# A sliding-window attention with a gated block on one core: first loads regrouped, block 0 handled in three pieces, five POOL drains

## The chip, the cores and the metric

The kernel runs on one core of a Trainium2 chip. The metric is device time in microseconds (us), the median of several executions. Every execution quoted here is fast, with a granted TensorE clock of 0.995 to 1.0. Engines are PE (matmul), PEld (its weight loads), DVE (vector), ACT (scalar), POOL (GpSimd) and SP (here only a queue that issues DMAs). All times inside an execution are counted from the start of its span, which is the stretch from the first to the last instruction of the profiled execution.

## The reference

```python
x = A_x                                   # (1, 2048, 512), bf16
xn = layernorm(x)                         # over the 512 columns, no weights
qkv = xn @ wqkv                           # 512 -> 3*512; 32 heads of 16
o = softmax(q k^T / 4, causal, window 256) v
h = (x @ w_gate) * (x @ w_up)             # 1792 wide; the kernel uses xn, see below
return x + o @ wo + h @ w_down
```

In the real text the second branch is called as `_B_ref(xn, ...)`, so both branches read the normalised `xn`. The output is 2048 x 512 in bf16. The tokens are handled in 4 chunks of 512 (`T`), each chunk in 4 blocks of 128 tokens (`b`).

## The kernel before

The kernel is written as a list of operations with dependencies. A small planner in Python walks the list while the kernel is built: it has estimates of when loads land and how long each operation takes, and it emits instructions in the order in which its plan starts them. The order on each engine is therefore fixed when the kernel is built, and the numbers of the plan decide it.

The first loads are issued on two queues, SP and ACT:

```python
load(nc.sync, self.Wqkv[:, 0:2, 1024:1536], ...)      # value weights, first half
load(nc.scalar, self.x[:, 0, :], xv[:, 0, :])         # x0: block 0 of x
load(nc.sync, self.Wqkv[:, 2:4, 1024:1536], ...)      # value weights, second half
load(nc.scalar, self.x[:, 1, :], xv[:, 1, :])         # x1
for t, lo in ((2, 512), (3, 0)):                      # key weights, x2; query weights, x3
    load(nc.sync, self.Wqkv[:, :, lo:lo + 512], ...)
    load(nc.sync, self.x[:, t, :], xv[:, t, :])
# ... gate and up weights, x4 to x15 ...
for f, g in ((0, 4), (4, 8), (8, 11), (11, 14)):
    load(nc.sync, self.Wd[:, f:g], w["d"][:, f:g])
load(nc.sync, self.Wo[:], w["o"])
for _ in range(4):
    nc.sync.drain()
# ... constants on POOL, DVE and ACT ...
nc.gpsimd.memset(self.V[0][:, :, :, 16:18], 1.0)
self.keep_busy(42, 0)                                 # 42 idle matmuls on PE
```

For every block of chunk 0 DVE takes statistics, ACT a square root, DVE a reciprocal, and DVE scales the block. PE turns it (four 128 x 128 transposes into a PSUM bank), and DVE or ACT copies the turned block to `xnT`. Then come the value, key and query matmuls. Keys are copied out twice ("lanes"), each time with half of the heads zeroed:

```python
land = (3.4, 3.95, 7.7, 9.6)              # the plan: when x0 to x3 land
wv, wk, wq = 5.9, 7.3, 9.3                # ... and value, key and query weights
# ...
parts = 2 if b == 0 else 1                # block 0 is scaled in halves
for n in range(parts):
    cols = slice(n * 512 // parts, (n + 1) * 512 // parts)
    # ... one op on DVE: i_apply(b, cols)
# ...
def k_out(o, i, b=b):                     # o: the matmuls, i: their bank
    x = o
    for lane in range(2):                 # lane 1 waits for lane 0
        x = self.op(f"K0b{b}", PSUM_COPY, [o, x], lambda e, lane=lane: self.i_keys(...))
    self.frees(x, i)                      # the bank is free after lane 1
# ...
for n, ks in enumerate(([0, 1], [2, 3]) if b == 0 else ([0, 1, 2, 3],)):
    self.A.insert(at + n, Dense(f"turn{b}", ...))     # block 0 is turned in halves
```

All turns, projections and later matmuls take one of four PSUM banks `M[0..3]`, whichever the plan has had free the longest:

```python
def take_bank(self):
    i = min((t, i) for i, t in enumerate(self.banks) if t is not None)[1]
    self.banks[i] = None
    return i
```

The last output block is summed and stored in two halves, the first on SP, the second on ACT:

```python
queue = "A" if cols.start else "S"
self.op(f"out{t}", {queue: (0.6, 2.2)}, [x], lambda e: (
    self.nc.scalar if cols.start else self.nc.sync).dma_start(
    out=self.out_d[128 * t:128 * t + 128, cols], in_=keep["y"][:, cols]), rank=0)
```

The softmax here doesn't subtract the row's maximum and nothing guards it: scores larger than these inputs give would overflow.

Of the kernel before, what the change touches and what calls it, by code (L numbers as in the profile page):

```python
# [50 lines left out]
def layout(T):  # L51


    if T == 0:
        return [[(2, 2, 4, 0), (4, 4, 4, 4)], [(0, 0, 5, 0), (5, 5, 3, 5)],
                [(1, 1, 5, 0), (6, 6, 2, 5), (7, 7, 1, 7)], [(3, 3, 5, 0), (2, 6, 1, 5)]]
    return [[(3, 3, 5, 0), (-3, 0, 2, 5), (-4, 0, 1, 7)], [(2, 2, 5, 0), (6, 6, 2, 5), (7, 7, 1, 7)],
            [(0, 0, 5, 0), (5, 5, 3, 5)], [(1, 1, 5, 0), (-2, 0, 3, 5)], [(-1, 0, 4, 0), (4, 4, 4, 4)]]
# [27 lines left out]
class Kernel:  # L86
# [56 lines left out]
    def prologue(self):  # L143
        nc = self.nc
        xv = self.x_d.rearrange("(t p) d -> p t d", p=128)
        w = {k: v.rearrange("(k p) n -> p k n", p=128) for k, v in self.w_d.items()}

        def load(eng, dst, src):
            eng.dma_start(out=dst, in_=src)  # L149

        load(nc.sync, self.Wqkv[:, 0:2, 1024:1536], w["qkv"][:, 0:2, 1024:1536])
        load(nc.scalar, self.x[:, 0, :], xv[:, 0, :])
        load(nc.sync, self.Wqkv[:, 2:4, 1024:1536], w["qkv"][:, 2:4, 1024:1536])
        load(nc.scalar, self.x[:, 1, :], xv[:, 1, :])
        for t, lo in ((2, 512), (3, 0)):
            load(nc.sync, self.Wqkv[:, :, lo:lo + 512], w["qkv"][:, :, lo:lo + 512])
            load(nc.sync, self.x[:, t, :], xv[:, t, :])
        h = self.F // 2
        for lo in (0, h):
            load(nc.sync, self.Wg[:, :, lo:lo + h], w["g"][:, :, lo:lo + h])  # L160
            load(nc.sync, self.Wu[:, :, lo:lo + h], w["u"][:, :, lo:lo + h])
            if lo == 0:
                load(nc.sync, self.x[:, 4:8, :], xv[:, 4:8, :])
        load(nc.sync, self.x[:, 8:NT, :], xv[:, 8:NT, :])
# [6 lines that stand above are left out]
        c = self.const  # L171
        nc.gpsimd.memset(self.ident[:], 0.0)
        nc.gpsimd.affine_select(out=self.ident[:], in_=self.ident[:], compare_op=ALU.not_equal, fill=1.0,
                                base=0, pattern=[[-1, 128]], channel_multiplier=1)
        nc.gpsimd.memset(self.mhalf[:], -0.5)
        warm = c.tile([128, 1], F32, name="warm")
        nc.vector.memset(warm[:], 0.0)
        nc.vector.memset(self.eps[:], 1e-5)
        nc.scalar.activation(out=warm[:], in_=warm[:], func=ACT.Sqrt)
        self.warm = warm  # L180
        pi = c.tile([128, 1], I32, name="pi")
        nc.gpsimd.iota(pi[:], pattern=[[0, 1]], base=0, channel_multiplier=1)
        podd = c.tile([128, 1], I32, name="podd")
        nc.vector.tensor_scalar(out=podd[:], in0=pi[:], scalar1=4, scalar2=1,
                                op0=ALU.arith_shift_right, op1=ALU.bitwise_and)
        nc.vector.tensor_copy(out=self.own[:, 1:2], in_=podd[:])
        nc.vector.tensor_scalar(out=self.own[:, 0:1], in0=podd[:], scalar1=0, scalar2=None, op0=ALU.is_equal)
        nc.gpsimd.memset(self.V[0][:, :, :, 16:18], 1.0)
        self.keep_busy(42, 0)


# [96 lines left out]
    def run(self):  # L288
        if self.live:
            self.prologue()  # L290
        self.now, self.mode = 5.4, "D"
        self.free = {"V": 3.0, "A": 4.5, "G": 3.0, "S": 6.0}
        self.waiting, self.log, self.idle = [], [], []
        self.banks = [0.0] * 4
        self.s_free, self.p_free = 0.0, [0.0] * self.PBUFS
        self.at_ = {}
        self.A, self.B = [], []
        self.g = self.v = 0
        self.first_s = None
        self.credit = 0.0  # L300
        self.pairs = [(T, c) for T in range(NCH) for c in range(4)]
        self.batches, self.of_pair = [], []
        for T, c in self.pairs:
            batches = layout(T)
            self.of_pair.append(range(len(self.batches), len(self.batches) + len(batches)))
            self.batches += [(T, c, b) for b in batches]
        self.list_work()
        self.loop()
        return max(self.now, *self.free.values(), *(o for o in self.at_.values() if isinstance(o, float)))
# [263 lines left out]
    def psT(self, i):  # L573
        return self.M[i].bitcast(BF16)[:, 0:512].rearrange("p (k t) -> p k t", k=4)

    def first_chunk(self):

        land = (3.4, 3.95, 7.7, 9.6)
        wv, wk, wq = 5.9, 7.3, 9.3
        nc = self.nc  # L580
        roots = []
        for b in range(4):
            keep = {}

            halves = 2 if b == 1 else 1

            def bn(e, n, b=b, keep=keep, halves=halves):
                if n == 0:
                    keep["st"] = self.work.tile([128, 2, 6], F32, tag="st", name="st")
                cols = slice(n * 512 // halves, (n + 1) * 512 // halves)  # L590
                nc.vector.bn_stats(out=keep["st"][:, n, :], in_=self.x[:, b, cols])  # L591
                if n == halves - 1:
                    nc.vector.bn_aggr(out=self.mv[0][:, b, :], in_=keep["st"][:, 0:halves, :])

            deps = [land[b]]
            for n in range(halves):
                took = (0.72 if halves == 1 else 0.38) + (0.14 if n == halves - 1 else 0)
                s = self.op(f"st{b}", {"V": (took, took + 0.04)}, deps, lambda e, n=n, bn=bn: bn(e, n), rank=0.5)
                deps = [self.at_["ap", 0, 0], s] if b == 1 else deps
            s = self.op(f"sq{b}", {"A": (0.24, 0.25)}, [s], lambda e, b=b: nc.scalar.activation(  # L600
                out=self.ve[:, b:b + 1], in_=self.mv[0][:, b, 1:2], func=ACT.Sqrt, bias=self.eps[:]), rank=0)
            roots.append(s)
            s = self.op(f"rs{b}", {"V": (0.15, 0.16)}, [s], lambda e, b=b: nc.vector.reciprocal(  # L603
                out=self.rs[0][:, b:b + 1], in_=self.ve[:, b:b + 1]), rank=0)
            parts = 2 if b == 0 else 1
            for n in range(parts):
                cols = slice(n * 512 // parts, (n + 1) * 512 // parts)
                took = (0.38, 0.48) if parts == 1 else (0.22, 0.30)
                self.at_["ap", b, n] = self.op(f"ap{b}", {"V": took}, [s], lambda e, b=b, cols=cols: self.i_apply(b, cols), rank=0)
        self.op("table", {"A": (1.5, 1.5)}, roots + [("Q", 0, 0, 2)], lambda e: nc.scalar.activation(  # L610
            out=self.warm[:], in_=self.warm[:], func=ACT.Exp), rank=1)
        last = self.op("masks", {"V": (0.15, 0.2)}, [self.at_["ap", 1, 0]], lambda e: nc.vector.memset(self.masks[:], -1), rank=9)
# [6 lines left out]
        for b in range(4):  # L619
            tok = slice(128 * b, 128 * b + 128)  # L620

            def turn(i, ks, b=b):
                for k in ks:
                    self.nc.tensor.transpose(self.psT(i)[:, k, :], self.xn[b][:, 128 * k:128 * k + 128], self.ident[:])  # L624
                if b == 0:
                    self.keep_busy(2 * ks[0], 3)

            def turned(o, i, ks, b=b, tok=tok):
                took = {"A": (0.48, 0.6), "V": (0.31, 0.41)} if len(ks) == 4 else {"A": (0.27, 0.38)}
                ks = slice(ks[0], ks[-1] + 1)  # L630
                x = self.op(f"xT{b}", took, [o], lambda e: self.copy(e, self.xnT[0][:, ks, tok], self.psT(i)[:, ks]), rank=0)
                self.frees(x, i)
                self.at_["xnT", 0, b] = self.at_["xnT", 0, b, ks.start] = x
                x.then.append(lambda o: self.at_.update({("begun", 0, b, ks.start): o.start}))
# [20 lines left out]
                    self.at_["Q", 0, c, b] = x  # L655

            at = len(self.A) - 2 if b else 0
            for n, ks in enumerate(([0, 1], [2, 3]) if b == 0 else ([0, 1, 2, 3],)):
                self.A.insert(at + n, Dense(f"turn{b}", 1.3 * len(ks) / 4, [("ap", b, n)], lambda i, f=turn, ks=ks: f(i, ks),
                                            lambda o, i, f=turned, ks=ks: f(o, i, ks)))  # L660
            self.add_v(0, b, wv)
# [171 lines left out]
```

## Time and profile before

| | before |
|---|---|
| time, median of 3 executions | 265.99 us (265.85 to 266.75) |
| time beside the change later, median of 6 | 265.89 us (265.64 to 266.75) |
| span of the profiled execution | 264.0 us |
| first value matmul / first key matmul of block 0 | 6.29 / 7.63 us |
| first score matmul | 17.33 us |
| end of DVE's last output sum | 261.03 us |
| from there to the end of the span ("the tail") | 2.95 us |

These lines are from the page of the kernel before: the span, each engine's busy time with its share and its instructions, the shares of the chain that ended last, and three of the DMA queues (packets, MB, share of 16 engines). Queues of the kind "instruction" fetch the program itself.

```profile
span 264.0 us, 8009 instructions
...
PE 259.4 (98%) x3456; PEld 131.9 (50%) x3456; DVE 190.6 (72%) x368; ACT 165.0 (63%) x122; POOL 119.7 (45%) x272
...
q8 instruction: 27, 0.44, 0.7%
q10 hardware_dynamic: 432, 0.33, 0.4%
q14 instruction: 8, 0.07, 0.1%
...
PE 96%; DMA 2%; DVE 1%; ACTq 0%; issue 0%
```

PE bounds the kernel, and the chain of waits is almost only PE. Before the first matmuls, other things decide.

The timeline of the kernel before (start, duration, engine, line, operation, out<-in, count; in brackets the idle time before it and what ended that). "SPq" and "ACTq" are the issues of DMAs.

```profile
3.41 0.69 DVE L591 BATCH_NORM_STATS2 st<-x 128x6 f32<-128x512 bf16 x1 [1.47 <-DMA x<-in_A_x_dram]
...
4.60 0.43 DVE L591 BATCH_NORM_STATS2 st<-x 128x6 f32<-128x256 bf16 x1 [0.29 <-DMA x<-in_A_x_dram]
4.95 0.15 DVE L603 RECIPROCAL rs<-ve 128x1 f32<-128x1 f32 x1
...
6.29 1.06 PE L689 MATMUL M<-Wqkv,xnT 128*64 128x256 bf16 x16
...
7.63 1.24 PE L207 MATMUL M<-xnT,Wqkv 128*128 128x128 bf16 x18
...
10.81 1.95 PE L207 MATMUL M<-xnT,Wqkv 128*128 128x128 bf16 x32
...
11.26 0.39 DVE L203 COPY xnT<-M 128x512 bf16<-128x512 bf16 x1
12.23 0.75 DVE L284 TENSOR_SCALAR K<-M,own 128x512 bf16<-128x512 f32 x1
...
17.33 0.40 PE L215 MATMUL S<-Q,K 32*128 32x256 bf16 x8
...
260.82 0.37 SPq L790 DMA_DIRECT2D out_dram<-xn  x1
261.06 0.35 ACTq L790 DMA_DIRECT2D out_dram<-xn  x1
```

DVE takes x1's statistics (4.60) before it does x0's reciprocal (4.95): the late x1 holds up block 0.

Busy time by stretch, where the last three columns are the granted clock, the DMA share and GB/s (the times of packets are added up, so a share can exceed 1):

```profile
core 0: us, PE busy (x) PEld busy (x) DVE busy (x) ACT busy (x) POOL busy (x), PEclk, DMA share, GB/s
3.00:4.00 1.00, 1.00 (x13) 1.00 (x11) 0.59 (x1) 0.22 (x2) 0.00 (x0) 1.00 1.08 360
4.00:5.00 1.00, 1.00 (x12) 1.00 (x11) 0.68 (x4) 0.29 (x1) 0.00 (x0) 1.00 1.06 351
```

```profile
out_dram<-xn SPq DMA_DIRECT2D x1, 64.0 KB, 1.6
out_dram<-xn ACTq DMA_DIRECT2D x1, 64.0 KB, 1.6
```

### The profile page before, as it was taken

To read this page: it belongs to the slowest core of one execution; us is meant where nothing else is said; L and a number is where in the kernel's file an instruction comes from. 1 tells how busy PE (TensorE), PEld (TensorE's weight loads), DVE (VectorE), ACT (ScalarE), POOL (GpSimd) and SP (SyncE) were. 2 spreads that over 40 slices of the span, in tenths; PEclk is the share of its full clock that TensorE was granted. 3 is DMA by queue.
4 is the path that set the end of the run, shared out by engine and by line. 5 is a ranking of instruction groups with operands and counts; after the bars stand their busy time and mean duration, and the time that the engine had idled before them with its cause. 6 is when DMAs were issued, how large, how long until landed. Compare 5 with 4: busy or idle time off the path is not lost.

```text
span 264.0 us, 8009 instructions
## 1 busy us (share of the span) xinstructions
PE 259.4 (98%) x3456; PEld 131.9 (50%) x3456; DVE 190.6 (72%) x368; ACT 165.0 (63%) x122; POOL 119.7 (45%) x272
## 2 busy tenths in 40 slices
PE   8999999999999999999999999999999999999994
PEld 7974444554444354455534354546535353545462
DVE  4999886978996548777997467786946268786504
ACT  3457576768776766687776767677777676572000
POOL 1406655475175635427084736437081828255000
PEclk9999999999999999999999999999999999999999
DMA  6999910000002200000005200000000100000002
GB/s 219 381 374 350 215 22 1 2 0 2 4 2 59 64 22 22 0 2 2 2 0 83 62 22 0 4 2 0 2 2 22 40 4 22 2 0 2 0 2 81
DMA packets 17251, 13.88 MB, mean 53 GB/s; under 512 B 7104, under 2 KB 17216, under 8 KB 17216
## 3 DMA queue, kind: packets, MB, share of 16 engines
q1 hardware_dynamic: 16784, 13.05, 18.0%
q8 instruction: 27, 0.44, 0.7%
q10 hardware_dynamic: 432, 0.33, 0.4%
q14 instruction: 8, 0.07, 0.1%
HBM read 9.70 MB, written 2.10 MB: 45 GB/s over the span
## 4 chain that ended last, share of the span: by engine, by line
PE 96%; DMA 2%; DVE 1%; ACTq 0%; issue 0%
PE M L207 72%; PE S L215 9%; PE M L245 7%; PE M L689 6%; DMA x<-in_A_x_dram 1%; DMA out_dram<-xn 1%; PE M L624 1%; PE S L207 1%; DVE xn L783 1%; DVE st L591 0%; ACTq L149 0%; DVE xn L273 0%; PE M L197 0%; DVE rs L603 0%
## 5 line engine op out<-in xcount | busy, mean ns | idle before, releaser
L498 ACT ACTIVATE P<-S 128x2048 bf16<-128x2048 f32 x76 | 140.9, 1854 | 57.1 <-PE S L215 50.5
L224 POOL TENSOR_SCALAR_AFFINE_SELECT P<-P 64x256 bf16<-64x256 bf16 (+1 forms) x248 | 112.6, 456 | 112.9 <-ACT P L498 100.7
L207 PE MATMUL M<-xnT,Wg 128*128 128x512 bf16 x224 | 57.7, 380 | 0.0
L207 PE MATMUL M<-xnT,Wu 128*128 128x512 bf16 x224 | 57.7, 380 | 0.0
L207 PE MATMUL M<-Wd,hT 128*128 128x512 bf16 (+1 forms) x224 | 51.8, 373 | 0.0
L741 DVE TENSOR_TENSOR hT<-M,gsb 128x512 bf16<-128x512 f32 x56 | 38.0, 678 | 8.4 <-PE M L207 8.1
L207 PEld LDWEIGHTS <-hT 128*128 128x128 bf16 x238 | 21.7, 98 | 23.4 <-issue 2.1
L207 PEld LDWEIGHTS <-Wu 128*128 128x128 bf16 x224 | 20.5, 98 | 24.8 <-issue 1.8
L207 PEld LDWEIGHTS <-Wg 128*128 128x128 bf16 x224 | 20.2, 98 | 24.3 <-issue 2.4
L203 DVE CAST gsb<-M 128x512 bf16<-128x512 f32 x41 | 28.1, 686 | 5.3 <-PE M L207 4.9
L207 PE MATMUL M<-xnT,Wqkv 128*128 128x128 bf16 (+1 forms) x224 | 30.3, 288 | 0.0
L215 PE MATMUL S<-Q,K 32*128 32x320 bf16 (+3 forms) x720 | 30.0, 254 | 0.0
L534 DVE STREAM_TRANSPOSE at<-M 128x512 f32<-128x512 f32 x32 | 21.3, 698 | 9.7 <-PE M L245 9.6
L215 PEld LDWEIGHTS <-K 32*128 32x128 bf16 x720 | 11.9, 92 | 31.8 <-issue 30.9
L230 DVE TENSOR_TENSOR P<-P,masks 128x512 int16<-128x512 int16 x56 | 22.6, 410 | 7.1 <-ACT P L498 7.1
L207 PEld LDWEIGHTS <-Wqkv 128*128 128x128 bf16 x224 | 15.9, 98 | 10.6 <-issue 1.5
L783 DVE TENSOR_TENSOR y<-M,x 128x512 bf16<-128x512 f32 x12 | 8.2, 687 | 16.5 <-PE M L207 16.3
L245 PE MATMUL M<-P,V 64*17 64x320 bf16 (+4 forms) x1440 | 19.5, 252 | 0.0
L245 PEld LDWEIGHTS <-V 64*17 64x17 bf16 x1440 | 17.1, 86 | 3.2 <-issue 1.3
L284 DVE TENSOR_SCALAR K<-M,own 128x512 bf16<-128x512 f32 x24 | 17.1, 743 | 2.1 <-PE M L207 2.1
L207 PE MATMUL M<-Wo,OT 128*128 128x512 bf16 (+1 forms) x64 | 16.6, 374 | 0.0
L689 PE MATMUL M<-Wqkv,xnT 128*64 128x256 bf16 x256 | 15.5, 274 | 0.0
(51 smaller groups left out, 138.0 us busy)
## 6 DMA issues: line engine op xcount, KB each, us to landing
Wg<-in_B_w_gate_dram SPq DMA_DIRECT2D x2, 896.0 KB, 10.2
Wu<-in_B_w_up_dram SPq DMA_DIRECT2D x2, 896.0 KB, 11.9
out_dram<-y SPq DMA_DIRECT2D x12, 128.0 KB, 1.7
Wqkv<-in_A_wqkv_dram SPq DMA_DIRECT2D x2, 512.0 KB, 6.1
x<-in_A_x_dram SPq DMA_DIRECT2D x1, 1024.0 KB, 13.6
Wd<-in_B_w_down_dram SPq DMA_DIRECT2D x2, 512.0 KB, 11.6
Wd<-in_B_w_down_dram SPq DMA_DIRECT2D x2, 384.0 KB, 8.7
Wqkv<-in_A_wqkv_dram SPq DMA_DIRECT2D x2, 256.0 KB, 3.5
```

The costliest lines, as they stand in the source:

```text
L203: self.nc.vector.tensor_copy(out=out, in_=in_)
L207: self.nc.tensor.matmul(ps, lhsT=a, rhs=b, start=first and n == 0, stop=last and n == len(pairs) - 1)
L215: self.nc.tensor.matmul(self.S[:, e, 64 * at:64 * (at + m)], lhsT=self.K[U % 3][rows, c, j].rearrange("p l t -> p (l t)"), rhs=self.Q[T % ...
L224: self.nc.gpsimd.affine_select(out=v, in_=v, pattern=[[0, 4], [0, n], [sign, 64]], base=0, fill=0.0, compare_op=ALU.is_gt if kind else ALU ...
L230: self.nc.vector.tensor_tensor(out=v, in0=v, in1=m, op=ALU.bitwise_and)
L245: self.nc.tensor.matmul(banks[lane][32 * e:32 * e + 17, 64 * q:64 * (q + m)], lhsT=self.V[U % 3][rows, j, 4 * c + e, 0:17], rhs=P[rows, e, ...
L284: self.nc.vector.tensor_scalar(out=out, in0=in_, scalar1=own, scalar2=None, op0=ALU.mult)
L498: ex = self.op(f"exp{g}", {"A": (took + 0.06, took + 0.18)}, [o], lambda e: self.nc.scalar.activation(out=P[:, :, 0:hi], in_=self.S[:, :, ...
L534: t = self.op(f"tr{v}", {"V": (0.63, 0.71)}, [o] + ts, lambda e, par=par: nc.vector.transpose(out=self.at[:, :, par, :], in_=self.M[banks[ ...
L689: self.nc.tensor.matmul(self.M[i][64 * lane:64 * lane + 64, 256 * jj:256 * jj + 256], lhsT=self.xnT[T % 2][:, k, tok], rhs=w[:, lane], sta ...
L741: x = self.op(f"u{T}.{f}", {"V": PSUM_COPY["V"]}, [o, ("gate", T, f)], lambda e: self.nc.vector.tensor_tensor(out=self.hT[T % 2][:, f, :], ...
L783: self.nc.vector.tensor_tensor(out=keep["y"][:, cols], in0=self.M[i][:, cols], in1=self.x[:, t, cols], op=ALU.add)
```

## The change

The intent is to start block 0 earlier. The first load of value weights is cut to a quarter, x1 moves from ACT's queue to the second place on SP, and three quarters of the value weights follow it. Block 0 is scaled, turned and copied in three pieces of 128, 128 and 256 columns instead of two halves. The plan gets new numbers, and POOL gets five drains.

```diff
-        load(nc.sync, self.Wqkv[:, 0:2, 1024:1536], w["qkv"][:, 0:2, 1024:1536])
+        load(nc.sync, self.Wqkv[:, 0:1, 1024:1536], w["qkv"][:, 0:1, 1024:1536])
         load(nc.scalar, self.x[:, 0, :], xv[:, 0, :])
-        load(nc.sync, self.Wqkv[:, 2:4, 1024:1536], w["qkv"][:, 2:4, 1024:1536])
-        load(nc.scalar, self.x[:, 1, :], xv[:, 1, :])
+        load(nc.sync, self.x[:, 1, :], xv[:, 1, :])
+        load(nc.sync, self.Wqkv[:, 1:4, 1024:1536], w["qkv"][:, 1:4, 1024:1536])
@@
         nc.gpsimd.memset(self.V[0][:, :, :, 16:18], 1.0)
+        for _ in range(5):
+            nc.gpsimd.drain()
         self.keep_busy(42, 0)
@@
-        self.now, self.mode = 5.4, "D"
-        self.free = {"V": 3.0, "A": 4.5, "G": 3.0, "S": 6.0}
+        self.now, self.mode = 4.8, "D"
+        self.free = {"V": 3.0, "A": 3.4, "G": 3.0, "S": 6.0}
@@
+    def parts(self, b):
+        return ([0], [1], [2, 3]) if b == 0 else ([0, 1, 2, 3],)
@@
-        land = (3.4, 3.95, 7.7, 9.6)
-        wv, wk, wq = 5.9, 7.3, 9.3
+        land = (3.3, 3.8, 7.9, 9.7)
+        wv, wk, wq = 5.2, 7.5, 9.35
@@
-            parts = 2 if b == 0 else 1
-            for n in range(parts):
-                cols = slice(n * 512 // parts, (n + 1) * 512 // parts)
+            for n, ks in enumerate(self.parts(b)):
+                cols = slice(128 * ks[0], 128 * ks[-1] + 128)
                 # (planned durations changed to match)
@@
                 if b == 0:
-                    self.keep_busy(2 * ks[0], 3)
+                    self.keep_busy(2, 3)
@@
-            for n, ks in enumerate(([0, 1], [2, 3]) if b == 0 else ([0, 1, 2, 3],)):
+            for n, ks in enumerate(self.parts(b)):
```

More of the change, by code (lines that the diff above doesn't have):

```diff
@@ L604, in first_chunk @@
                 out=self.rs[0][:, b:b + 1], in_=self.ve[:, b:b + 1]), rank=0)
-            parts = 2 if b == 0 else 1
-            for n in range(parts):
-                cols = slice(n * 512 // parts, (n + 1) * 512 // parts)
-                took = (0.38, 0.48) if parts == 1 else (0.22, 0.30)
-                self.at_["ap", b, n] = self.op(f"ap{b}", {"V": took}, [s], lambda e, b=b, cols=cols: self.i_apply(b, cols), rank=0)
+            for n, ks in enumerate(self.parts(b)):
+                cols = slice(128 * ks[0], 128 * ks[-1] + 128)
+                took = 0.06 + 0.08 * len(ks)
+                self.at_["ap", b, n] = self.op(f"ap{b}", {"V": (took, took + 0.08)}, [s],
+                                               lambda e, b=b, cols=cols: self.i_apply(b, cols), rank=0)
         self.op("table", {"A": (1.5, 1.5)}, roots + [("Q", 0, 0, 2)], lambda e: nc.scalar.activation(
@@ L625, in turn @@
                 if b == 0:
-                    self.keep_busy(2 * ks[0], 3)
+                    self.keep_busy(2, 3)
             def turned(o, i, ks, b=b, tok=tok):
-                took = {"A": (0.48, 0.6), "V": (0.31, 0.41)} if len(ks) == 4 else {"A": (0.27, 0.38)}
+                took = {"A": (0.48, 0.6), "V": (0.31, 0.41)} if len(ks) == 4 else {"A": (0.13 + 0.07 * len(ks), 0.22 + 0.07 * len(ks))}
                 ks = slice(ks[0], ks[-1] + 1)
```

## The prediction

> **What bounds the kernel.** The page gives PE 259.4 of 264.0 us (98%), and the chain of waits is 96% PE. PE's idle share hardly tells the whole story, because ends of matmuls are modelled (the Trainium skill, "Perfetto Trace Analysis", says the same of TensorE's end times), so I read starts. From the first score matmul (17.33 us) on, no start-to-start gap in the trace's order of instructions is a wait: the 0.31 us ones are all changes of tile mode behind a 512-column matmul. So the time is a constant plus the moment at which PE gets there, and only the first 17 us can change. The granted clock is 1.00 there.
>
> **The first 17 us before (timeline).** x0 lands at 3.41; its stats end 4.10. The next DVE instruction, half of x1's stats, waits for x1 (4.58) and holds up x0's reciprocal to 4.95. Scaling 5.13 to 5.73, first turn on PE 5.53, value matmuls of block 0 from 6.29, turn 1 at 7.39, key matmuls of block 0 (K0) at 7.59. The key weights land at about 7.5, the query weights 9.35, x2 7.91, x3 9.70. After that PE follows the copies: K of block 1 starts at 8.60 right behind the copy of turned block 1 (8.55), turn 2 at 10.57 behind the scaling of block 2 (10.52), K of block 2 at 11.70 right behind the copy of turned block 2 (11.65).
>
> **What the change does.** x1 should land near 3.9, so the reciprocal moves to about 4.65 and scaling to 4.8. The 42 idle matmuls end near 5.2 and become a floor; the turn starts at 5.2, value matmuls about 5.75 instead of 6.29, turn 1 about 7.2. That is 0.5 us, but K0 still needs the key weights: the same 768 KB stand in front of them and DMA share is already 1.0 from 4 us (SP and ACT queues share the 16 engines: the Trainium skill, "Trainium Kernel Development and Optimization", Key Constraints). So K0 at about 7.5: 0.1 us gained. Three DVE pieces for two, one more ACT copy and two more idle matmuls cost about 0.2 us of DVE/ACT time, hidden. The five drains sit where POOL waits for 6 us: nothing.
>
> **What else it moves.** The start times in the kernel's own plan differ, so the order of DVE differs: the second lane of K of block 1 now stands before the copy of turned block 2, and waits for ACT's first lane. With durations of the trace: K lane 0 of block 0 on DVE ends at 9.6 (before 10.00), ACT's two lanes at 10.9 (before 11.30), DVE's lane 11.65, the copy 11.95 (before 11.65). PE, which could start K of block 2 at about 11.4, waits to about 12.0: 0.3 us later than before. Everything behind keeps its distance (the query copy moved to DVE and the mask fill stay hidden), so the first score comes at about 17.6, and the span at about 264.3.
>
> **Predicted: 266.25 us, 265.6 to 266.8 (8 in 10).** Faster by over 2%: 0.005; within 2%: 0.99; slower by over 2%: 0.005.
>
> **Right if:** the timeline shows value matmuls at 5.7 to 5.9, K0 at 7.4 to 7.6, DVE's K lane between mean/variance of block 3 and the copy of block 2, a PE gap of 0.4 to 0.7 us before 12.0, the first score at 17.5 to 17.8. **Wrong if:** the copy of block 2 comes by 11.5 (then 0.2 to 0.3 us are gained); the smaller first loads let the key weights and x2 land much earlier; x1 lands no earlier than 4.5; the drains shift instruction fetches into a stall; or PE waits newly after 17 us.

## More of the kernel before

From 10.81 PE runs 32 projection matmuls without a break, over the copy of turned block 2 at 11.26. At the end SP issues the first half of the last block at 260.82, and ACT the second half at 261.06. The DMA issues of the last microseconds are shown with KB each and us from issue to landing.

## The result and the profile after

| | before | after |
|---|---|---|
| time, median of 6 | 265.89 us (265.64 to 266.75) | 267.52 us (267.01 to 267.57) |
| ratio | | 1.0053 (95%: 1.0037 to 1.0069) |
| span of the profiled execution | 264.0 us | 265.3 us |
| x0 / x1 landed | 3.39 / 4.58 us | 3.58 / 3.82 us |
| last value weights / key weights landed | 5.11 / 7.54 us | 6.30 / 7.78 us |
| first value / first key matmul of block 0 | 6.29 / 7.63 us | 6.26 / 7.82 us |
| first score matmul | 17.33 us | 17.93 us |
| end of the last output sum | 261.03 us | 261.63 us |
| tail | 2.95 us | 3.64 us |
| of it, to the landing of the last output / after that | 1.66 / 1.29 us | 2.74 / 0.91 us |

A ratio is the mean time of one kernel's fast executions over that of the other's of the same rounds, so it is not quite the ratio of the medians. The change is slower by half a per cent; this is real, but within 2%. The profiled execution of the changed kernel is its fastest one (267.01 us), so the profile shows 1.3 us where the medians show 1.63 us.

In the profile the sum is simple: 0.60 us are lost before the first scores and stay lost unchanged up to the last sum (261.03 to 261.63), and 0.69 us are lost after the last sum. The last row splits the tail further: the last output lands 1.08 us later behind its sum, and what follows the landing (drains, and waits for semaphores, the counters by which engines wait for each other, that close the program) is 0.38 us shorter.

The same lines of the changed kernel's page. PE has 3423 records against 3458 weight loads, where the kernel before has 3456 of each: 35 records of matmuls are missing from this trace. The lower busy time of PE comes mostly from that: the trace of e14 below, with all 3458 records, has 258.9 us. Part of the lower share in the chain may come from it too.

```profile
span 265.3 us, 7984 instructions
...
PE 256.5 (97%) x3423; PEld 131.9 (50%) x3458; DVE 191.3 (72%) x370; ACT 164.7 (62%) x122; POOL 120.0 (45%) x272
...
q10 hardware_dynamic: 288, 0.20, 0.3%
q14 instruction: 10, 0.08, 0.1%
...
PE 92%; DVE 3%; DMA 2%; issue 1%; ACT 0%
```

The timeline of the changed kernel:

```profile
3.61 0.69 DVE L597 BATCH_NORM_STATS2 st<-x 128x6 f32<-128x512 bf16 x1 [1.67 <-DMA x<-in_A_x_dram]
...
4.88 0.16 DVE L609 RECIPROCAL rs<-ve 128x1 f32<-128x1 f32 x1
...
6.26 1.06 PE L695 MATMUL M<-Wqkv,xnT 128*64 128x256 bf16 x16
...
7.82 1.07 PE L209 MATMUL M<-xnT,Wqkv 128*128 128x128 bf16 x16
...
10.83 1.06 PE L209 MATMUL M<-xnT,Wqkv 128*128 128x128 bf16 x16
...
11.18 0.75 DVE L286 TENSOR_SCALAR K<-M,own 128x512 bf16<-128x512 f32 x1
11.85 0.41 DVE L205 COPY xnT<-M 128x512 bf16<-128x512 bf16 x1
12.31 0.66 PE L209 MATMUL M<-xnT,Wqkv 128*128 128x128 bf16 x9 [0.42 <-DVE xnT L205]
...
17.93 0.40 PE L217 MATMUL S<-Q,K 32*128 32x256 bf16 x8
...
261.66 0.35 ACTq L796 DMA_DIRECT2D out_dram<-xn  x1
261.83 0.33 SPq L796 DMA_DIRECT2D out_dram<-xn  x1
```

x1 no longer holds up the reciprocal, but the reciprocal comes only 0.07 us earlier, and the value matmuls only 0.03 us. The 32 projection matmuls from 10.81 are now broken in two, with a gap before 12.31; DVE's second key lane of block 1 (11.18) stands before the copy of turned block 2 (11.85). And at the end SP's issue comes at 261.83, after ACT's, although its half was summed first.

The stretches in which the first loads land, for the changed kernel (columns as before):

```profile
3.00:4.00 1.00, 1.00 (x13) 1.00 (x11) 0.39 (x1) 0.00 (x0) 0.00 (x0) 1.00 0.65 157
4.00:5.00 1.00, 1.00 (x12) 1.00 (x11) 0.92 (x4) 0.29 (x1) 0.00 (x0) 1.00 0.60 184
5.00:6.00 1.00, 0.89 (x13) 0.59 (x11) 0.96 (x5) 0.28 (x2) 0.00 (x0) 1.00 1.07 372
6.00:7.00 1.00, 1.00 (x19) 0.82 (x20) 0.57 (x3) 0.79 (x3) 0.00 (x0) 1.00 1.08 375
```

From 3 to 5 us the DMA engines are no longer full: the share falls from 1.08 and 1.06 to 0.65 and 0.60. By 4.5 us the packets in the trace have brought 470 KB, before 741 KB. From 5 us on the same queue, still alone, fills the engines (1.07 and 1.08).

The last DMA issues of the changed kernel take longer to land than the 1.6 us of before:

```profile
out_dram<-xn ACTq DMA_DIRECT2D x1, 64.0 KB, 2.1
out_dram<-xn SPq DMA_DIRECT2D x1, 64.0 KB, 2.5
```

Among these packets fall two instruction fetches. This is the view of DMA queues over the 0.8 us from 262.4 us of the changed kernel, in which the last outputs move:

```profile
q10 hardware_dynamic: 140, 0.06, 27.7%
q1 hardware_dynamic: 126, 0.06, 25.0%
q14 instruction: 2, 0.02, 9.9%
```

In the kernel before, the same view over 261.6 to 262.26 us, which holds nearly all packets of its last outputs, shows no instruction fetch; its first one of the end starts at 262.27 us:

```profile
q1 hardware_dynamic: 164, 0.08, 39.8%
q10 hardware_dynamic: 143, 0.07, 34.6%
```

### The profile page after: what moved, and what is told of

Its sections match the earlier page's. It is cut to its first block, busy times and chain, and to the rows that moved or that the text cites. A ratio compares the mean times of both kernels' runs of the same rounds, so it can differ in the third digit from the quotient of the medians.

```text
span 265.3 us, 7984 instructions
## 1 busy us (share of the span) xinstructions
PE 256.5 (97%) x3423; PEld 131.9 (50%) x3458; DVE 191.3 (72%) x370; ACT 164.7 (62%) x122; POOL 120.0 (45%) x272
## 4 chain that ended last, share of the span: by engine, by line
PE 92%; DVE 3%; DMA 2%; issue 1%; ACT 0%
PE M L209 69%; PE S L217 9%; PE M L247 7%; PE M L695 5%; DMA x<-in_A_x_dram 1%; DVE st L597 1%; DMA out_dram<-xn 1%; PE S L209 1%; DVE xn L789 1%; DVE K L286 1%; DVE xn L275 0%; PE M L630 0%; DVE xnT L205 0%; DVE V L205 0%; DVE mv L599 0%
## 5 line engine op out<-in xcount | busy, mean ns | idle before, releaser
L209 PE MATMUL M<-xnT,Wu 128*128 128x512 bf16 x216 | 56.8, 380 | 0.3
L209 PE MATMUL M<-Wd,hT 128*128 128x512 bf16 (+1 forms) x216 | 50.5, 373 | 0.9 <-issue 0.8
L209 PE MATMUL M<-Wo,OT 128*128 128x512 bf16 (+1 forms) x60 | 15.7, 373 | 0.5 <-issue 0.5
```

Source lines behind the costliest of these rows:

```text
L209: self.nc.tensor.matmul(ps, lhsT=a, rhs=b, start=first and n == 0, stop=last and n == len(pairs) - 1)
```

## The experiments

All were correct against the reference. "Before" in a row is the kernel before on the same chip in the same rounds. The questions were these:

- The start: is the 0.6 us lost because the order on DVE puts the copy of block 2 behind the key lane (as predicted), because of the loads, or because of something else that the pieces move?
- The end: do POOL's drains shift instruction fetches into the last outputs, does the additional DMA on SP disturb the queue, or is it simply the number of instructions on SP?

| run | first score | last sum | tail | median (before) | ratio (95%) |
|---|---|---|---|---|---|
| e1, change without POOL drains | 17.96 | 261.66 | 4.31 | 268.07 (265.65) | 1.0094 (1.0080 to 1.0108) |
| e2, before + POOL drains | 17.48 | 261.18 | 2.83 | 265.43 (265.65) | 0.9993 (0.9979 to 1.0007) |
| e3, before + new loads | 18.59 | 262.28 | 3.68 | 267.45 (265.65) | 1.0065 (1.0053 to 1.0078) |
| e4, before + pieces and plan | 17.89 | 261.59 | 2.88 | 266.29 (265.65) | 1.0027 (1.0015 to 1.0040) |
| e5, new loads on two queues | 17.40 | 261.10 | 2.89 | 266.37 (265.62) | 1.0018 (1.0006 to 1.0030) |
| e6, only x1 to SP | 17.53 | 261.22 | 3.97 | 266.90 (265.62) | 1.0051 (1.0039 to 1.0063) |
| e7, only quarters for halves | 18.05 | 261.74 | 2.93 | 265.95 (265.62) | 1.0018 (0.9998 to 1.0038) |
| e8, before, output weights in two loads | 17.59 | 261.29 | 3.67 | 266.46 (265.62) | 1.0028 (1.0015 to 1.0041) |
| e9, e4 with lane behind copy | 17.89 | 261.59 | 2.89 | 266.32 (265.78) | 1.0019 (1.0005 to 1.0032) |
| e10, change, 3 SP drains for 4 | 18.71 | 262.40 | 2.50 | 266.12 (265.78) | 1.0009 (0.9994 to 1.0024) |
| e11, change, one SP load fewer | 17.91 | 261.60 | 2.50 | 266.08 (265.78) | 1.0009 (0.9995 to 1.0022) |
| e12, pieces, drains, other order | 17.29 | 260.99 | 2.44 | 265.28 (265.78) | 0.9981 (0.9967 to 0.9995) |
| e13, before + 1 SP drain | 17.42 | 261.12 | 3.65 | 266.46 (265.69) | 1.0022 (1.0007 to 1.0037) |
| e14, change, 3 SP drains, no POOL drains | 19.09 | 262.78 | 2.91 | 266.80 (265.69) | 1.0037 (1.0018 to 1.0056) |

The first three columns of times are from one profiled execution each, the medians from 5 or 6. In every run the last sum lies 243.7 us behind the first score (within 0.01 us): nothing between 17 and 261 us changed in any of them. Single executions spread at the start: before, e2, e8 and e13 have the same instructions there up to POOL's drains, and their first score came at 17.33 to 17.59 us. So a difference of 0.1 or 0.2 us in the first column says little.

### First set: the parts alone

**e1_nodrain.**

```diff
-        for _ in range(5):
-            nc.gpsimd.drain()
```

> The changed kernel without its five POOL drains. Three losses are seen in the traces of the change: the first score matmul comes 0.6 us later (17.93 for 17.33), and from the end of the last DVE sum to the end of the span it takes 3.6 us for 3.0. Theory T (the drains shift POOL's instruction fetches so that one meets the last output transfers): the first score stays at 17.9, the tail falls back to about 3.0, time near 266.5. Rival U (the tail comes of the moved load: SP has one instruction more, ACT one fewer): the tail stays at 3.6 or more, time near 267.5. Rival C (the tail is chance): the tail differs from run to run without order.

Measured: 268.07 us, which is 2.42 us over its kernel before, where the change itself is 1.63 us over its own: 0.8 us worse without the drains. The tail is 4.31 us. So the drains do not cause the late end; they make the tail shorter.

**e2_bdrain.** The five drains in the kernel before, and nothing else.

```diff
+        for _ in range(5):
+            nc.gpsimd.drain()
```

> The kernel before with the five POOL drains added and nothing else. Theory T: first score at 17.33 as before, tail 3.6 us or more, time 266.6 to 266.9. Rival U: tail 3.0, time 265.9, the same as before.

Measured: 265.43 us, tail 2.83 us. The interval of the ratio holds 1. The theory that drains push fetches into the last outputs has fallen.

**e3_loads.** The four load lines of the change, and nothing else.

> The kernel before with the four first loads as in the change and nothing else; the instructions of PE, DVE and POOL stand exactly as before. Theory (one queue alone leaves the DMA engines dry from 3.3 to 4.8 us): DMA share well under 0.8 in that stretch, key weights land at 7.8 for 7.5, key matmuls of block 0 at 7.8, first score at 17.4 to 17.6, since the copy of turned block 2 does not wait for the key lane in this order. Time 266.0 to 266.2 with a tail of 3.0. Rival U says the tail is 3.6 here as well, and the time 266.7 or more. If the loads were good as they were meant, the first score would come before 17.3.

Measured: 267.45 us. In the profiled execution the key weights land at 9.04 us instead of 7.54, the first score comes at 18.59 us, and the tail is long (3.68 us). The view of waits (of whom for whom: us in total, times, longest) has PE wait for the weights, which it does not do in the kernel before:

```profile
PE M L207 <- DMA Wqkv<-in_A_wqkv_dram: 1.3, 1, 1.3
```

So the loads bring both a late start and the late end.

**e4_pieces.** The pieces and the plan's numbers, with the loads of before and no drains. The order on every engine is that of the change.

```diff
+    def parts(self, b):
+        return ([0], [1], [2, 3]) if b == 0 else ([0, 1, 2, 3],)
         # and every other hunk of the change except the loads and the POOL drains
```

> The kernel before with block 0 in three pieces and the new start times of the plan (which alone change no instruction), loads and drains as before; the order on DVE is that of the change. Theory (third piece takes a third bank, the banks rotate differently, and the plan puts the second lane of the keys of block 1 before the copy of turned block 2): key weights land at 7.5, copy of turned block 2 ends at 12.0 to 12.3 for 11.65, a PE gap of 0.4 to 0.6 us before it, first score at 17.6 to 17.9, time near 266.3 with a tail of 3.0. Rival (the order is harmless and the stall comes of the late loads alone): first score at 17.3.

Measured: 266.29 us, first score 17.89 us, tail 2.88 us. The pieces alone bring nearly all of the 0.6 us at the start, and none of the end. Building (not running) the kernel before with the plan's new numbers alone gave exactly the old order, so it is the third piece that reorders, by taking one bank more.

### Second set: which part of the loads

**e5_two.** The change's loads, but the three quarters of the value weights go to ACT's queue. SP then issues as many instructions as before.

```diff
-        load(nc.sync, self.Wqkv[:, 1:4, 1024:1536], w["qkv"][:, 1:4, 1024:1536])
+        load(nc.scalar, self.Wqkv[:, 1:4, 1024:1536], w["qkv"][:, 1:4, 1024:1536])
```

> The kernel before with x1 second on SP behind the first quarter of the value weights, and the other three quarters behind x0 on ACT: both queues are fed, and SP has as many loads as before. Theory Q (the loads of the change lose because one queue alone feeds the DMA engines): no dry stretch between 3.3 and 4.8 us, key weights land by 7.5, first score at 17.4 or sooner. Theory N (the late tail comes of one load more on SP): SP's last output is issued within 0.2 us of its sum, the tail is 2.8 to 3.0. Time 265.3 to 265.9. If x1 on SP were itself at fault, the loss of 1 us or more stays.

Measured: the DMA engines stay full, as the same two stretches show for this run, and in the profiled execution start and end are as before (17.40 and 2.89 us):

```profile
3.00:4.00 1.00, 1.00 (x14) 1.00 (x12) 0.26 (x1) 0.22 (x2) 0.00 (x0) 1.00 1.06 304
4.00:5.00 1.00, 0.76 (x13) 0.58 (x10) 0.93 (x3) 0.29 (x1) 0.00 (x0) 1.00 1.10 374
```

The time is less clear: two executions took 265.70 and 265.73 us and three took 266.37 to 266.53 us, against 265.62 us before; the profile is one of the first two. What makes the others slow is open.

**e6_x1sp.** Halves as before, only x1 moved to the second place on SP.

```diff
+        load(nc.sync, self.x[:, 1, :], xv[:, 1, :])
         load(nc.sync, self.Wqkv[:, 2:4, 1024:1536], w["qkv"][:, 2:4, 1024:1536])
-        load(nc.scalar, self.x[:, 1, :], xv[:, 1, :])
```

> The kernel before with only x1 moved from second on ACT to second on SP, between the two halves of the value weights. Theory Q: the DMA engines run dry once x0 is through, as with all loads of the change; key weights land at 7.8 or later, first score at 17.5 to 18.6. Theory N: tail 3.5 to 3.7, SP's last output is issued only when the second last but one has landed. Time 266.5 to 267.5. Rival S (it is the split into a quarter and three quarters that loses): as before, 265.7.

Measured: 266.90 us, first score 17.53 us, tail 3.97 us. The long tail comes with one more DMA on SP. The DMA share is 1.01 and 0.83 in the two stretches, so the shortage is milder with halves, and it comes later (0.72 from 5 to 6 us).

**e7_split.** A quarter and three quarters on SP, x0 and x1 on ACT as before.

```diff
-        load(nc.sync, self.Wqkv[:, 0:2, 1024:1536], w["qkv"][:, 0:2, 1024:1536])
+        load(nc.sync, self.Wqkv[:, 0:1, 1024:1536], w["qkv"][:, 0:1, 1024:1536])
         load(nc.scalar, self.x[:, 0, :], xv[:, 0, :])
-        load(nc.sync, self.Wqkv[:, 2:4, 1024:1536], w["qkv"][:, 2:4, 1024:1536])
+        load(nc.sync, self.Wqkv[:, 1:4, 1024:1536], w["qkv"][:, 1:4, 1024:1536])
```

> The kernel before with only the split changed: first quarter, then three quarters of the value weights on SP, x0 and x1 on ACT as before. Theories Q and N: key weights land at 7.5, first score at 17.3, tail 3.0, time 265.4 to 265.9, the same as before. Rival S: a dry stretch and 266.5 or more.

Measured: x1 lands at 5.31 us, so the value matmuls start at 7.02 us and the first score comes at 18.05 us, while the key weights land early (6.90 us). The tail stays at 2.93 us: the sizes of the loads do not cause it. The six executions spread from 265.49 to 267.56 us, and the interval of the ratio holds 1.

**e8_wo2.** The kernel before, with the last load on SP cut in two, so SP issues one DMA more, far from the start.

```diff
-        load(nc.sync, self.Wo[:], w["o"])
+        load(nc.sync, self.Wo[:, 0:2], w["o"][:, 0:2])
+        load(nc.sync, self.Wo[:, 2:4], w["o"][:, 2:4])
```

> The kernel before with the last weight load on SP cut in two, so that SP issues one load more, late, where nothing waits for it. Theory N as a matter of the number of instructions or DMAs on SP: first score at 17.33, tail 3.5 or more, time 266.3 to 266.7. If the tail needs the 128 more rows that x1 brings to SP's queue, or comes of the timing of the first loads, the tail stays at 3.0 and the time at 265.7.

Measured: 266.46 us, tail 3.67 us. One DMA more on SP is enough for the long tail, with the first loads as they were.

### Third set: banks, and the end mended

**e9_defer.** e4 with the second key lane of block 1 emitted right behind the copy of turned block 2, to test the order on DVE.

```diff
-                        e, 0, slice(0, 4), lane, ...)
+                        # for block 1, lane 1: held back, emitted after the copy of block 2
```

> The kernel with the three pieces alone (it took 0.64 us more than before, first score 17.89), in which the second lane of the keys of block 1 is written one place later on DVE, behind the copy of turned block 2; no other instruction moves. If the order on DVE is the cause, as the prediction put it, the first score returns to 17.4 and the time to 265.7. Rival B (the bank): the keys of block 2 are written to the very bank from which that lane is read, so PE waits for the lane wherever it stands: lane ends at 12.2 to 12.4, PE gap as before, first score at 17.8 to 18.0, time near 266.3.

Measured: no change against e4 (first score 17.89 us, 266.32 us). The timeline of this run shows why:

```profile
11.17 0.39 DVE L203 COPY xnT<-M 128x512 bf16<-128x512 bf16 x1
...
11.48 0.74 DVE L284 TENSOR_SCALAR K<-M,own 128x512 bf16<-128x512 f32 x1
...
12.27 0.83 PE L207 MATMUL M<-xnT,Wqkv 128*128 128x128 bf16 x12 [0.49 <-DVE K L284]
```

The copy is done at 11.56 us, and PE still waits until the key lane is done (12.22 us). The trace names what ended that wait, the key lane, but leaves bank numbers out; the banks are read from the kernels as built (not run for this). In the change, in e4 and in e9 the keys of block 1 stand in `M[2]`, and the keys of block 2 are written into `M[2]` as well, while the second lane is still being read from it. In the kernel before they stand in `M[1]` and go into `M[3]`. So PE's wait is for the bank, and the order on DVE was not what held it.

**e10_sp3.** The change, with three SP drains instead of four: SP has one DMA more than before, and the old number of instructions.

```diff
-        for _ in range(4):
+        for _ in range(3):
             nc.sync.drain()
```

> The changed kernel with three drains on SP in place of four, so that SP has as many instructions as the kernel before but still one DMA more. If the late tail is a matter of SP's instruction count (where its fetch falls): SP's last output is issued within 0.2 us of its sum, tail 2.7 to 3.0, time 0.7 us less than the change, 266.7 to 266.9. If it is a matter of the number of DMAs on SP: last output still waits for the landing of the second output, tail 3.6, time 267.4.

Measured: 266.12 us, tail 2.50 us, although the key weights landed late in the profiled execution (8.69 us, first score 18.71 us). The outputs at the end land in 1.6 us each again, SP's at once behind its sum. The time is 0.6 us below what I had expected, in part because the drains shorten the tail as well.

**e11_wd3.** The change, with the last two loads of `Wd` joined: one DMA fewer on SP.

```diff
-        for f, g in ((0, 4), (4, 8), (8, 11), (11, 14)):
+        for f, g in ((0, 4), (4, 8), (8, 14)):
```

> The changed kernel with the last two of four loads of the down weights joined, so that SP has one DMA (and one instruction) fewer: as many DMAs on SP as before. Both readings of the tail: tail 2.7 to 3.0, SP's last output issued before ACT's, time 266.6 to 266.9; the first score stays near 17.9. If it stays at 267.4, the number of DMAs is not the cause either.

Measured: 266.08 us, tail 2.50 us, first score 17.91 us. Two quite different edits that both take one instruction from SP mend the end, and take 1.3 us of the 1.63 us by the medians (266.08 − 265.78 = 0.30 us remain).

**e12_fix.** e4 with the five POOL drains, the second key lane of block 1 put behind the copy of turned block 2 (as a dependency, so that the plan gives other banks), the queries of block 0 copied by ACT alone, and the mask fill after the scaling of block 3. Loads as before.

```diff
-                    x = self.op(f"K0b{b}", PSUM_COPY, [o, x], lambda e, lane=lane: self.i_keys(
+                    x = self.op(f"K0b{b}", PSUM_COPY, [o, x] + ([("xnT", 0, 2)] if (b, lane) == (1, 1) else []), lambda e, lane=lane: self.i_keys(
@@
-                x = self.op(f"Q0b{b}", PSUM_COPY, [o], lambda e: self.copy(
+                x = self.op(f"Q0b{b}", PSUM_COPY if b else {"A": PSUM_COPY["A"]}, [o], lambda e: self.copy(
@@
-        last = self.op("masks", {"V": (0.15, 0.2)}, [self.at_["ap", 1, 0]], ...
+        last = self.op("masks", {"V": (0.15, 0.2)}, [self.at_["ap", 3, 0]], ...
```

> What the runs point to: the first loads of the kernel before, block 0 in three pieces, the five drains, and the keys of block 1 kept off DVE (second lane on ACT after the copy of turned block 2, first queries on ACT), so that the keys of block 2 go to a bank that is free by 11.6. First score at 17.2 to 17.5, tail 2.7 to 3.0, time 265.2 to 265.6, at most 0.4 us better than before, since the key weights still land at about 7.5.

Measured: 265.28 us, the best of all, 0.19% under the kernel before, with an interval that excludes 1. The timeline of this run shows PE without the gap again:

```profile
10.70 2.03 PE L209 MATMUL M<-xnT,Wqkv 128*128 128x128 bf16 x32
...
11.69 0.69 ACT L284 ACTIVATE K<-M,own 128x512 bf16<-128x512 f32 x1
```

The key lane still runs (now on ACT, at 11.69 us), and PE does not wait for it, since the keys of block 2 have another bank (`M[3]`; those of block 1 are in `M[2]`). The pieces and the drains are therefore not bad in themselves: the first score is at 17.29 us and the tail is 2.44 us. Nearly all of the gain is in the tail (2.95 to 2.44 us); the 0.04 us at the start is within the spread of single executions.

### Fourth set: what of SP, beyond twelve runs

After twelve runs the cause of the late end was still open in two points: whether the number of SP's instructions is enough without any other DMA, and what the POOL drains do when the end is in order.

**e13_sp5.** The kernel before with a fifth drain on SP, nothing else: the same DMAs, one instruction more.

```diff
-        for _ in range(4):
+        for _ in range(5):
             nc.sync.drain()
```

> The kernel before with a fifth drain on SP (23 us into the kernel, where SP then waits for work) and nothing else: one instruction more on SP, no DMA more. If the instruction count of SP alone sets the late tail: first score at 17.3, SP's last output issued only when the second output has landed, tail 3.6 to 4.0, time 0.6 to 0.9 us over the kernel before. If the additional DMA is needed as well: tail 2.9, same time as before.

Measured: 266.46 us against 265.69, tail 3.65 us. The medians differ by 0.77 us, the ratio of the means is worth 0.6 us, and the tails differ by 0.70 us. The timeline of this run, to be compared with 260.82 (SP) and 261.06 (ACT) of before:

```profile
261.15 0.35 ACTq L790 DMA_DIRECT2D out_dram<-xn  x1
261.32 0.33 SPq L790 DMA_DIRECT2D out_dram<-xn  x1
```

One drain at the end of the loads, some 240 us earlier, makes SP's last issue late and costs 0.77 us by the medians. No other instruction of the program differs, on any engine. So one instruction more on SP is enough, whether it is a DMA or not. Only one more and one fewer were tried.

**e14_sp3nod.** The change with three SP drains and no POOL drains.

```diff
-        for _ in range(4):
+        for _ in range(3):
             nc.sync.drain()
@@
-        for _ in range(5):
-            nc.gpsimd.drain()
```

> The changed kernel with three drains on SP in place of four and without the five POOL drains, to size the POOL drains where SP is in order: with them it took 266.12 us, tail 2.5. If they only take POOL's fetch out of the end of the kernel: tail 2.9, time 266.4 to 266.6. If they work through SP's late output only (0.6 to 0.8 us there), they do nothing here: tail 2.5, time 266.1.

Measured: 266.80 us, tail 2.91 us; the key weights landed at 9.08 us in the profiled execution. With e1, e10 and the change itself this gives a square. All four have the change's loads and pieces; tail in us and, in brackets, the ratio to the kernel before:

| | SP as the change has it | SP one instruction fewer |
|---|---|---|
| without POOL drains | 4.31 (1.0094) | 2.91 (1.0037) |
| with POOL drains | 3.64 (1.0053) | 2.50 (1.0009) |

The SP instruction costs 1.14 to 1.40 us of tail, and the drains give back 0.41 to 0.67 us. The four ratios agree in direction with it; they come from different chips, and late key weights vary within them.

## Why the prediction was right or wrong

The direction and the class were right (slower, within 2%). The time was not: predicted 266.25 us with a range up to 266.8, measured 267.52.

**The step that failed** is this: "So the time is a constant plus the moment at which PE gets there, and only the first 17 us can change." The first half held: the first score, the last sum and everything between kept one distance of 243.7 us in all runs. But the 2.95 us behind the last sum were not a constant. They became 3.64 us in the profile, and with the end mended by one instruction less on SP (e10, e11) the change measures 266.12 and 266.08 us, inside the predicted range. The end of the kernel is the term that was sized at zero and measured +0.69 us in the profile. That is a sum of two: the SP instruction lengthens the tail by 1.14 us (2.50 in e10 and e11, 3.64 in the change), and the POOL drains shorten it by 0.45 us (2.95 before, 2.50 in e10 and e11). By the medians, taking the SP instruction away is worth about 1.3 us (1.63 − 0.30 for e11 and − 0.34 for e10).

*What happens at the end.* The load lines put one DMA more on SP and one fewer on ACT. In all runs with one SP instruction more and without a compensation (the change, e1, e3, e6, e8, e13; 90 instructions of SP in the trace), SP issues its last output 0.54 to 0.55 us behind its sum, after ACT's. In the other ten runs (89 instructions) it does so 0.13 to 0.14 us behind the sum, before ACT's. The late issue falls together with the landing of the second of SP's outputs of the last chunk: 261.83 and 261.82 us in the change, 261.32 and 261.31 in e13, and as close in the other four. But the end runs on the same pattern in all of them, so a wait for that landing can't be told from a fixed delay. The program's own waits do not explain it: in the change the semaphore wait before the issue is over at 261.37 us, and the sum that the issue waits for ended at 261.28. Nor does the trace show a fetch of instructions that lands between 254 and 262.4 us. Why the count of earlier instructions moves the issue, no run shows; that stays open.

In the six runs with the late issue the last outputs take 2.1 to 2.75 us to land instead of about 1.6 us, with instruction fetches of 8 KB among their packets; in the other ten, at most a tenth of ACT's packets come after the first fetch, and none of SP's. With one fetch among the packets (e3, e6, e8, e13) the last output lands 2.30 to 2.61 us behind the last sum, with two (the change, e1) 2.74 to 2.96, and in the other ten 1.59 to 1.69. The fetch as the reason of the slow landing fits these numbers, also that the SP instruction costs more in the changed kernel; it was not tested by itself.

**The start: +0.6 us where +0.3 was predicted.** The picture of the gap was right: DVE's key lane stands before the copy of block 2 (they start at 11.18 and 11.85 us; predicted to end at 11.65 and 11.95, measured 11.93 and 12.26), and PE waits just before 12.31 us (predicted about 12.0). The cause that I named was the copy's place in DVE's order. e9 put it back in front and gained nothing; PE then waited for the lane itself. The cause is the bank: the third piece takes one bank more, which turns the rotation, so that the keys of block 2 are to be written where the keys of block 1 are still read. The change in order came from the same rotation, so the two could not be told apart by reading. e12, with other banks, has the first score at 17.29 us. So here both were off: the mechanism, and the size, since the steps before it were late as well (key lane 0 of block 0 ended at 9.84 us, predicted 9.6).

**The loads.** x1 was predicted near 3.9 us and landed at 3.82. But "value matmuls about 5.75" measured 6.26, and "K0 at about 7.5" measured 7.82. The step that failed is "DMA share is already 1.0 from 4 us": this was the share of the kernel before, with two queues at work. The change leaves SP's queue alone after x0, with two loads of 128 KB in front, and the share falls to 0.65 and 0.60 from 3 to 5 us. That one queue is alone is not enough for it: SP's queue fills the engines alone from 5 us in the change, and before it did so from 4.2 us. That the first loads on SP are small may matter as much; no run separates the two. x0 itself landed 0.19 us later in the profiled execution, and its statistics began 0.20 us later, which used up most of the gain there; but x0 landed at 3.28 to 3.65 us in the runs with before's loads and at 3.45 to 3.64 in those with the change's, so this is not clear of the spread. The three pieces did not shorten the rest: from the start of the scaling to the value matmuls it took 1.18 us (5.08 to 6.26) after 1.16 us before (5.13 to 6.29), where I had put 0.95. It is so in e4 too, with before's loads: 1.18 us. The value matmuls stand behind the third turn in PE's order, and that one began only at 5.93, behind the scaling, whose three pieces take DVE until 5.87. So the "about 0.2 us of DVE/ACT time, hidden" of the prediction was not hidden here.

The prediction leaned there on the Trainium skill, "Trainium Kernel Development and Optimization", section "Key Constraints", that the queues of SP, ACT and POOL share 16 DMA engines and that "issuing from several engines concurrently only saves the sequencer's issue time". The traces agree that they share: before, SP's queue q1 had 71.9% of the engines' time from 3.6 to 4.2 us while ACT's queue q10 had 34.6%, and 105.6% from 4.2 to 5 us, when q10 was done. They do not agree that only issue time is saved in this stretch: e5 differs from e3 in the queue of one load, and has a share of 1.06 and 1.10 and 304 and 374 GB/s, where e3 moves 173 and 174 GB/s.

How much the late weights cost by themselves is uncertain. With the change's own load lines (the change, e1, e3, e10, e11, e14) the key weights landed at 7.78, 7.90, 9.04, 8.69, 7.88 and 9.08 us in the one profiled execution of each; with before's (before, e2, e4, e8, e9, e12, e13) at 6.76 to 7.99. Where they land by 7.9 us with the change's loads and pieces, the first score is at 17.91 to 17.96, about as with the pieces alone (17.89), so the wait for the bank seems to hide them. Where they land at 8.7 us or later, the first score goes to 18.59 to 19.09. In e3, 1.80 us in all minus the 0.77 us of one SP instruction (e13) leaves an estimate of 1.0 us; from e11 only some 0.1 us (0.30 − 0.64 for the pieces + 0.45 for the drains).

**The drains: "nothing".** They do something, and it is a gain: 0.41 us of tail with SP in order (e14 to e10), 0.67 us with SP late (e1 to the change). Most of it lies behind the landing of the last output: from there to the end of the span it takes 1.29 to 1.36 us in all runs without drains and 0.85 to 0.91 us in those with drains and pieces; in e2, with drains alone, 1.14 us. So fetches among the outputs are not what the drains mainly change. The individual packets show one fetch of 8 KB near 238 us in every run with drains (238.26 in the change) and none there without them; without drains one more fetch lies near the end. This fits a fetch of POOL being moved forward from the end, but which engine a packet belongs to is inferred from the drains that move it. "Wrong if: the drains shift instruction fetches into a stall" had the right object and the wrong sign, and it missed that SP's own count could do it.

**What held.** From the first score to the last sum there was no new wait, and in e12 the additional pieces, copies and idle matmuls do not show at the first score (17.29 us). Reading PE by starts rather than by busy time was also right: the Trainium skill, "Perfetto Trace Analysis", section "Tensor Engine Instruction (MATMUL, LD_WEIGHTS)", says that the profiler estimates the end of a TensorE instruction, and here PE's busy time *fell* from 259.4 to 256.5 us in the slower kernel, mostly because of missing records.

**The account in time.** Roughly, from medians (and, for the lower figure of the drains, tails): pieces +0.64 us (e4), one SP instruction +0.77 us (e13), the loads' landing somewhere between 0.1 and 1.0 us, POOL drains −0.4 to −0.8 us. The sum of these estimates spans the measured +1.63 us, but the parts do not add exactly (the SP instruction costs more in the changed kernel than in the one before), and I do not claim a finer split.

## What to carry to other kernels

The end of a kernel is not a constant even if nothing near it was edited: look at when each queue issues its last outputs, and try one instruction more or less on that queue before blaming the start. Split the tail at the landing of the last output, since what comes after it can change too. A piece more in a pool of few PSUM banks turns the rotation for everything after it, so look for who still reads the bank that a waiting matmul will write, and test it by changing the bank, not only the order. When loads are moved between queues, check the DMA share stretch by stretch: it shows where the engines run dry.

## What the Trainium skill lacked or had wrong

- "Runtime: NRT & Kernel Launch", section "Instruction fetch mechanics", says that a refill of 16 KiB costs "one DMA tail-bump, mostly hidden". The queue q8, by its size PE's, agrees on the block (27 packets of 16 KB, 0.44 MB). The other instruction queue moves packets of 8,192 bytes, one at a time (8 to 10 packets, 0.07 to 0.08 MB). And not all is hidden: five POOL drains shortened the tail from 2.91 to 2.50 us (e14 to e10) while one 8 KB fetch moved away from the end; that the fetch is the reason is inferred.
- No page says that one instruction more on SP can delay SP's last DMA issue: one drain, and nothing else, cost 0.77 us (266.46 against 265.69 us, e13), with the issue 0.55 us behind its sum instead of 0.14 us. The mechanism is open.
- "Trainium Kernel Development and Optimization", section "Key Constraints", says that issuing from several engines only saves issue time. From 3 to 5 us of this kernel that was not all: one load moved from SP's queue to ACT's (e3 to e5) raised the rate from 173 and 174 to 304 and 374 GB/s. From 5 us on, one queue alone filled the engines (a share of 1.07 and 1.08 in the change), as the page has it.
